# A linear-attention block: q tiles spread over the state stage, the first normaliser block inside it, and the folded Wo written to memory and read back by head groups

## Chip, cores, metric

One core of one Trainium2 chip. The metric is the device time of one execution in microseconds (us), the median of several. The profile's *span*, from the first to the last instruction, is a little shorter than the time. Positions "at 79.4" are us from the start of the span. TensorE multiplies, VectorE (DVE) and ScalarE (ACT) do elementwise work, and the sync engine's queue (SPq) issues most transfers.

## The reference, cut to what matters

```python
B, S, D = 1, 2048, 640;  H = 32;  Dh = 20
q, k, v = split(x @ wqkv)                    # [B, H, S, Dh] each
phi = lambda t: where(t > 0, t + 1, exp(t)) + 1e-6
pq, pk = phi(q), phi(k)
kv  = einsum("bhsd,bhse->bhde", pk, v)       # the state, per head
z   = einsum("bhsd->bhd", pk)
num = einsum("bhqd,bhde->bhqe", pq, kv)
den = einsum("bhqd,bhd->bhq", pq, z)[..., None] + 1e-6
out = (num / den merged over heads) @ wo
```

## The kernel before

It never forms v. TensorE computes K and phi(K) (16 tiles, `k_tile`), then the state stage `P = x^T phi(K)` in two halves of 16 steps (`p_step`), then `kv = Wv^T P` for groups of 6 heads (`kv_group`), and multiplies each group's kv into its rows of Wo (`w2_group`). This *folded Wo* is copied to the tile `w2g`, written to a DRAM buffer `w_rows`, and read back with its rows in another order into `w2p`: the *Wo round trip*. phi(Q) is made in 20 *q tiles* (`q_tile`: five 512-column matmuls, an exp on ScalarE, two VectorE operations) that fill gaps. The normaliser of each of four blocks of 512 rows is a small matmul (`den`), a reciprocal on ScalarE (`den_act`), a spreading matmul (`den_spread`), and five multiplications on VectorE (`normalize`). The sums over phi(K) that z needs are made on VectorE too (the *z additions*), and P is copied out of its banks into `pt`. At the end come 16 output tiles, each of which needs all of `w2p`.

Semaphore waits are derived from what each operation reads and writes. Every engine runs its list in order, and so does the issuing queue: an issue that waits holds back every issue behind it.

```python
# ... cut: loads, z additions, kv_group
def w2_rows():                      # after the last w2_group
    P.add("sp", lambda e: e.dma_start(
        w2d[0:5 * GW, :].rearrange("(g p) n -> p g n", p=GW),
        w2g[0:GW, 0:5 * D].rearrange("p (g n) -> p g n", n=D)), ..., dma=True)
    P.add("sp", lambda e: e.dma_start(w2d[5 * GW:D, :], w2g[0:gsz[5], 5 * D:6 * D]), ...)
    for c in range(NC_):            # five reads, 128 partitions each
        P.add("sp", lambda e, c=c: e.dma_start(
            w2p[:, c * D:(c + 1) * D],
            w2d.rearrange("(h c j) n -> c h j n", c=NC_, j=4)[c]), ..., dma=True)

# ... cut: the schedule. 16 warm-up matmuls on zeros, 16 K tiles, then
for h in range(2):
    for st in range(NT):
        p_step(h, st)
        if zst and st % 2 == 1:
            zst.pop(0)()            # one z addition on VectorE
        if st == 7:
            next_q(5 + qi[0] % 3)   # one q tile
    p_out(h)                        # evacuates banks 0..4: 3 copies ACT, 2 DVE ("pt")
    next_q(...); next_q(...)
kv_group(0)
# ... cut: six w2_groups among six q tiles, then w2_rows(); eight more q tiles
#          with den, den_spread and normalize of blocks 1 and 2; 16 output tiles
```

## Time and profile before

| | before |
|---|---|
| time, median of 4 | 110.6 us (110.52 to 110.74) |
| span of the profiled run | 109.2 us |
| first K matmul | 8.04 us |
| last matmul ends | 106.43 us |
| TensorE idle in between | 3.64 us |
| last w2g copy ends, w2p complete | 71.78, 81.32 us |

The last two rows come from the trace: the copy's record, and the last completion increment of the last read.

From the profile's page of before, its span in 40 slices, busy share in tenths (PEclk: granted TensorE clock in tenths):

```profile
PE   5949999999979999999999999994999879999990
...
PEclk9999999999999999999999999999999999999999
DMA  1999999999991000000000000074550131333333
```

TensorE is full nearly everywhere; the clock is full; the transfers come at the start and again from slice 26 (the Wo round trip and the stores). So TensorE bounds this kernel, and a change that removes no matmul can win only idle time. The timeline of TensorE of before shows that idle time: start, duration, engine, line, operation, and in brackets the idle time just before it and what ended it.

```profile
8.04 21.89 PE L237 MATMUL ps<-wk,xT 128*128 128x320 bf16 x160 [1.43 <-DMA xT<-in_x_dram]
...
30.59 5.61 PE L261 MATMUL ps<-pk,xn 128*128 128x320 bf16 x40 [0.66 <-DVE pk L252]
...
75.36 3.41 PE L287 MATMUL ps<-xT,wqp 128*128 128x512 bf16 x14 [1.52 <-DVE pq L300]
...
82.56 2.88 PE L446 MATMUL ps<-w2p,pq 128*128 128x320 bf16 x20
...
88.59 17.83 PE L446 MATMUL ps<-w2p,pq 128*128 128x320 bf16 x130 [0.68 <-ACT rd L430]
```

The first output tile (82.56) follows q work without a gap: the round trip is hidden, by a margin of 1.2 us. The queue's timeline of before has it as two writes and five reads:

```profile
70.47 0.34 SPq L387 DMA_DIRECT2D w_rows<-w2g  x1
71.81 0.29 SPq L391 DMA_DIRECT2D w_rows<-w2g  x1
76.05 3.16 SPq L395 DMA_DIRECT2D w2p<-w_rows  x5
```

### The profile page before, as it was taken

Reading aid. Unit: us, or ns where it says so; the run is one execution under the profiler, and the core shown is the slowest. Engines: PE = TensorE matmul, PEld = TensorE weight load, DVE = VectorE, ACT = ScalarE, POOL = GpSimd, SP = SyncE. Lnnn points to the kernel's source line nnn. Section 1 sums busy time; section 2 is a strip of 40 time slices with the busy share of each in tenths; the row PEclk is TensorE's granted clock in tenths of the full one; section 3 lists DMA queues with packets and bytes.
Section 4 is the critical chain, followed back from the end, with each engine's and each line's share of the span. In section 5 each row is a group of like instructions: output and inputs, shape, how many; then the busy total and the mean of one; then the engine's idle time right before and its main releaser. Section 6 shows DMA issues by size and latency. Waiting matters only on the chain.

```text
span 109.2 us, 1857 instructions
## 1 busy us (share of the span) xinstructions
PE 100.1 (92%) x738; PEld 64.2 (59%) x744; DVE 66.7 (61%) x132; ACT 41.4 (38%) x77; POOL 10.2 (9%) x25
## 2 busy tenths in 40 slices
PE   5949999999979999999999999994999879999990
PEld 2317777777657676576766756451446557777760
DVE  1002888888899899910306675899879674333331
ACT  3102555555520203400107269873566543333330
POOL 7870000480000000000000000000000000000000
PEclk9999999999999999999999999999999999999999
DMA  1999999999991000000000000074550131333333
GB/s 32 242 270 264 221 190 253 382 362 363 314 199 42 0 0 0 3 0 0 6 0 0 3 0 0 6 178 122 145 155 0 50 136 60 120 120 120 127 121 118
DMA packets 19499, 12.90 MB, mean 118 GB/s; under 512 B 10915, under 2 KB 19491, under 8 KB 19491
## 3 DMA queue, kind: packets, MB, share of 16 engines
q1 hardware_dynamic: 18178, 11.96, 39.7%
q10 hardware_dynamic: 1312, 0.82, 2.8%
q8 instruction: 6, 0.10, 0.4%
q14 instruction: 3, 0.02, 0.1%
HBM read 6.72 MB, written 3.44 MB: 93 GB/s over the span
## 4 chain that ended last, share of the span: by engine, by line
PE 72%; DVE 13%; DMA 6%; ACT 5%; issue 1%
PE ps L237 19%; PE ps L446 18%; PE ps L261 15%; PE ps L287 15%; DMA xT<-in_x_dram 6%; DVE za L306 4%; DVE pq L300 3%; ACT eq L295 3%; DVE pq L437 2%; PE ps L405 2%; PE ps L356 1%; DVE eq L297 1%; ACT rd L430 1%; PE ps L337 1%; PE ps L377 1%
## 5 line engine op out<-in xcount | busy, mean ns | idle before, releaser
L287 PE MATMUL ps<-xT,wqp 128*128 128x512 bf16 x94 | 22.9, 379 | 1.8 <-DVE pq L300 1.5
L237 PE MATMUL ps<-wk,xT 128*128 128x320 bf16 x160 | 21.9, 299 | 1.4 <-DMA xT<-in_x_dram 1.4
L261 PE MATMUL ps<-pk,xn 128*128 128x320 bf16 x160 | 22.4, 299 | 0.8 <-DVE pk L252 0.7
L446 PE MATMUL ps<-w2p,pq 128*128 128x320 bf16 x160 | 22.2, 299 | 0.7 <-ACT rd L430 0.7
L237 PEld LDWEIGHTS ps<-wk,xT 128*128 128x128 bf16 x160 | 15.6, 98 | 7.9 <-issue 1.9
L261 PEld LDWEIGHTS ps<-pk,xn 128*128 128x128 bf16 x160 | 15.5, 98 | 7.9 <-DVE pk L252 1.0
L295 ACT ACTIVATE eq<-ps 128x512 bf16<-128x512 f32 x20 | 11.9, 597 | 21.4 <-PE ps L287 21.3
L446 PEld LDWEIGHTS ps<-w2p,pq 128*128 128x128 bf16 x160 | 15.5, 98 | 7.0 <-ACT rd L430 0.8
L247 ACT ACTIVATE ek<-ps 128x640 bf16<-128x640 f32 x16 | 11.3, 704 | 16.3 <-PE ps L237 16.3
L287 PEld LDWEIGHTS ps<-xT,wqp 128*128 128x128 bf16 x100 | 9.3, 98 | 11.0 <-DVE pq L300 1.9
L455 DVE CAST osb<-ps 128x320 bf16<-128x320 f32 x16 | 7.8, 490 | 11.5 <-PE ps L446 11.5
L300 DVE SCALAR_TENSOR_TENSOR pq<-ps,eq 128x512 bf16<-128x512 f32 x20 | 13.8, 692 | 0.7
L252 DVE SCALAR_TENSOR_TENSOR pk<-ps,ek 128x640 bf16<-128x640 f32 x16 | 13.2, 825 | 0.5
L297 DVE TENSOR_SCALAR eq<-eq 128x512 bf16<-128x512 bf16 x20 | 5.8, 292 | 10.9 <-ACT eq L295 10.4
L249 DVE TENSOR_SCALAR ek<-ek 128x640 bf16<-128x640 bf16 x16 | 5.4, 339 | 11.5 <-ACT ek L247 11.3
L453 ACT CAST osb<-ps 128x320 bf16<-128x320 f32 x16 | 6.8, 426 | 13.2 <-PE ps L446 13.1
L437 DVE TENSOR_TENSOR pq<-pq,rd 128x512 bf16<-128x512 bf16 x20 | 7.0, 418 | 0.3 <-ACT rd L430 0.3
L228 PE MATMUL ps<-zero 128*128 128x512 bf16 x16 | 5.3, 509 | 1.3 <-DVE eps L149 1.3
L273 ACT CAST pt<-ps 128x320 bf16<-128x320 f32 x6 | 2.2, 434 | 9.7 <-PE ps L261 9.7
L306 DVE TENSOR_TENSOR za<-pk 128x1280 f32<-128x1280 bf16 x4 | 5.7, 1484 | 0.0
L220 POOL COPY wqp<-wqn 128x640 bf16<-128x640 bf16 x5 | 3.6, 756 | 12.7 <-DMA wqn<-in_wqkv_dram 12.7
L306 DVE TENSOR_TENSOR za<-za 128x1280 f32<-128x1280 f32 x3 | 4.4, 1487 | 0.0
(35 smaller groups left out, 39.9 us busy)
## 6 DMA issues: line engine op xcount, KB each, us to landing
xn<-in_x_dram SPq DMA_DIRECT2D x4, 640.0 KB, 9.1
out_dram<-osb SPq DMA_DIRECT2D x16, 160.0 KB, 1.8
wk<-in_wqkv_dram ACTq DMA_DIRECT2D x2, 400.0 KB, 5.5
wqn<-in_wqkv_dram SPq DMA_DIRECT2D x1, 800.0 KB, 5.2
wv<-in_wqkv_dram SPq DMA_DIRECT2D x1, 800.0 KB, 13.3
w2p<-w_rows SPq DMA_DIRECT2D x5, 160.0 KB, 2.7
wog<-in_wo_dram SPq DMA_DIRECT2D x1, 750.0 KB, 13.9
w_rows<-w2g SPq DMA_DIRECT2D x1, 750.0 KB, 5.3
```

Source lines behind the costliest of these rows:

```text
L237: r = e.matmul(bank(b + h, HALF), xT[:, c * S + 128 * st:c * S + 128 * st + 128], wk[:, c * D + HALF * h:c * D + HALF * (h + 1)], start=(c ...
L247: P.add("act", lambda e: e.activation(fold(t[:, :]), two_banks(b), ACTF.Exp), reads=banks + ["table"], writes=[("ek", st % 3)])
L252: P.add("dve", lambda e: e.scalar_tensor_tensor(fold(pk[:, st * D:(st + 1) * D]), two_banks(b), 0.0, fold(t[:, :]), ALU.max, ALU.add), rea ...
L261: r = e.matmul(bank(d, HALF), xn[:, st * D + 128 * d:st * D + 128 * d + 128], pk[:, st * D + HALF * h:st * D + HALF * (h + 1)], start=(st ...
L287: r = e.matmul(bank(b), wqp[:, d * D + 128 * c:d * D + 128 * c + 128], xT[:, d * S + BK * sbk:d * S + BK * (sbk + 1)], start=(d == 0), sto ...
L295: P.add("act", lambda e: e.activation(t[:, :], bank(b), ACTF.Exp), reads=[("bank", b), "table"], writes=[("eq", i)])
L297: P.add("dve", lambda e: e.tensor_scalar(t[:, :], t[:, :], 1.0, 1e-6, ALU.min, ALU.add), reads=[("eq", i)], writes=[("eq", i)])
L300: P.add("dve", lambda e: e.scalar_tensor_tensor(pq[:, c * S + BK * sbk:c * S + BK * (sbk + 1)], bank(b), 0.0, t[:, :], ALU.max, ALU.add), ...
L306: P.add("dve", lambda e: e.tensor_tensor(d_ap, a, b, ALU.add), reads=ra + rb, writes=[dst])
L437: P.add("dve", lambda e, v=v: e.tensor_tensor(v, v, rd[i][:, :], ALU.mult), reads=[("rd", i), ("pq", sbk, c)], writes=[("pq", sbk, c)])
L446: r = e.matmul(bank(b + h, HALF), pq[:, c * S + 128 * st:c * S + 128 * st + 128], w2p[:, c * D + HALF * h:c * D + HALF * (h + 1)], start=( ...
L455: P.add("dve", lambda e: e.tensor_copy(osb[j][:, HALF:D], bank(b + 1, HALF)), reads=[("bank", b + 1)], writes=[("osb", j, 1)])
```

## The change

Its intent: spread the q tiles over the state stage so that VectorE's work on them is even, do the first block's normaliser there, hand the normalising multiplications out one per q tile, and start the Wo round trip earlier, group by group. The edit holds more than its summary: x rows 0 to 255 now come by plain loads and are transposed on TensorE, with fewer warm-up matmuls; and the mask step stores kv with its columns in another order, so that a group's folded rows come out as five runs of 24.

```diff
+        NPE = 2          # cut: x tiles 0, 1 loaded first, transposed on TensorE,
+                         # K tiles 0, 1 done half by half; warm(16) -> warm(5), warm(4)
-        def w2_rows():   # cut, see above
+        def w2_write(g):
+            w = gsz[g] // NC_
+            P.add("sp", lambda e: e.dma_start(
+                w2d.rearrange("(c r) n -> c r n", c=NC_)[:, 24 * g:24 * g + w, :],
+                w2g[0:gsz[g], g * D:(g + 1) * D]), reads=[("w2g", g)], ..., dma=True)
+        def w2_read(g):
+            w = gsz[g] // NC_
+            P.add("sp", lambda e: e.dma_start(
+                w2p[24 * g:24 * g + w, :].rearrange("p (c n) -> p c n", n=D),
+                w2d.rearrange("(c r) n -> r c n", c=NC_)[24 * g:24 * g + w]),
+                reads=[("w2d", g)], ..., dma=True)
@@ the schedule, cut @@
+        p_step(0, 0, range(4)); p_step(0, 1, range(4))    # bank 4 later
+        p_step(0, 0, (4,));     p_step(0, 1, (4,))
+        for st in range(2, NT):
+            p_step(0, st)
+            if st % 2 == 1: zst.pop(0)()
+            if st in (3, 6, 9, 12): next_q()
+        p_out(0); next_q(); next_q()
+        for st in range(NT):
+            p_step(1, st)
+            if st == 3: z_finish(take())
+            if st == 6: inverse(0)       # den and den_act of block 0
+            if st == 9: spread(0)
+            if st in (4, 7, 10, 12): next_q()   # each also does one normalising piece
+        p_out(1); next_q(); next_q()
+        kv_group(0); next_q()
+        w2_group(0, 2); w2_write(0); inverse(1); next_q()
+        w2_group(1, 0); w2_write(1); w2_read(0)
+        w2_group(2, 2); w2_write(2); w2_read(1); spread(1); next_q()
+        w2_group(3, 0); w2_write(3); w2_read(2)
+        w2_group(4, 2); w2_write(4); w2_read(3); next_q()
+        w2_group(5, 0); w2_write(5); w2_read(4); w2_read(5)
+        # cut: four q tiles, den and spread of block 2, then the output tiles
```

More of the change, by code (lines that the diff above doesn't have):

```diff
@@ L124, in bass_standalone__linear_attn_block__prompt_kernel @@
         eps = sb("eps", 8, F32)
+        ident = sb("ident", 128)
         zero = sb("zero", BK)
@@ L147, in pool_const @@
             P.add("dve", lambda e: e.memset(zero[:, :], 0.0), writes=["zero"])
+            P.add("pool", lambda e: e.memset(ident[:, :], 0.0), writes=["ident"])
+            P.add("pool", lambda e: e.affine_select(
+                out=ident[:, :], in_=ident[:, :], pattern=[[-1, 128]], base=0,
+                channel_multiplier=1, compare_op=ALU.not_equal, fill=1.0),
+                reads=["ident"], writes=["ident"])
             P.add("dve", lambda e: e.memset(ones[:, :], 1.0), writes=["ones"])
@@ L172, in pool_const @@
                      0 if lo else DH - 1, 1 if lo else -1, "bm")
-        XCH = [(0, 256), (256, 512), (512, 1024), (1024, 1536), (1536, 2048)]
+        NPE = 2
+        XCH = [(0, 128), (128, 256), (256, 512), (512, 1024), (1024, 1536), (1536, 2048)]
         def xch_of(row):
@@ L179, in load_xT, with transpose_x, mm @@
         def load_xT():
-            for i, (a, b) in enumerate(XCH):
+            for i, (a, b) in enumerate(XCH[NPE:]):
                 P.add("sp", lambda e, a=a, b=b: e.dma_start_transpose(
                     xT[:, :].rearrange("p (c s) -> p c s", s=S)[:, :, a:b], x[0, a:b, :]),
-                    writes=[("xT", i)], dma=True)
+                    reads=[("xn", 0)] if i == 0 else [],
+                    writes=[("xT", NPE + i)], dma=True)
+        def transpose_x(st, b):
+            v = bank(b, HALF).bitcast(BF16)
+            def mm(e):
+                for c in range(NC_):
+                    r = e.transpose(v[:, 128 * c:128 * c + 128],
+                                    xn[:, st * D + 128 * c:st * D + 128 * c + 128], ident[:, :])
+                return r
+            P.add("pe", mm, reads=[("xn", st), "ident"], writes=[("bank", b)])
+            P.add("dve", lambda e: e.tensor_copy(
+                xT[:, :].rearrange("p (c s) -> p c s", s=S)[:, :, 128 * st:128 * st + 128],
+                v.rearrange("p (c s) -> p c s", s=128)),
+                reads=[("bank", b)], writes=[("xT", st)])
         def xT_keys(a, b):
@@ L192, in w_cols, with load_xn @@
                 writes=[key], dma=True)
+        def load_xn(a, b, eng):
+            P.add(eng, lambda e: e.dma_start(
+                xn[:, a * D:b * D].rearrange("p (t n) -> p t n", n=D),
+                x[0, 128 * a:128 * b, :].rearrange("(t p) n -> p t n", p=128)),
+                writes=[("xn", t) for t in range(a, b)], dma=True)
         def load_wk():
+            for t in range(NPE):
+                load_xn(t, t + 1, "act")
             w_cols(wk, 0, HALF, D, ("wk", 0), "act")
@@ L203, in load_rest @@
             w_cols(wqn, 0, D, 0, "wqn", "sp")
-            for q in range(4):
-                P.add("sp", lambda e, q=q: e.dma_start(
-                    xn[:, 4 * q * D:4 * (q + 1) * D].rearrange("p (t n) -> p t n", n=D),
-                    x[0, 512 * q:512 * (q + 1), :].rearrange("(t p) n -> p t n", p=128)),
-                    writes=[("xn", q)], dma=True)
+            for a, b in ((NPE, 4), (4, 8), (8, 12), (12, 16)):
+                load_xn(a, b, "sp")
             w_cols(wv, 0, D, 2 * D, "wv", "sp")
@@ L228, in warm, with k_half, mm, k_phi @@
                 P.add("pe", lambda e: e.matmul(
-                    bank(7), zero[:, 0:128], zero[:, :], start=True, stop=True),
-                    reads=["zero"], writes=[("bank", 7)])
-        def k_tile(st):
+                    bank(4), zero[:, 0:128], zero[:, :], start=True, stop=True),
+                    reads=["zero"], writes=[("bank", 4)])
+        def k_half(st, h):
             b = 2 * (st % 4)
-            for h in range(2):
-                def mm(e, h=h):
-                    for c in range(NC_):
-                        r = e.matmul(
-                            bank(b + h, HALF),
-                            xT[:, c * S + 128 * st:c * S + 128 * st + 128],
-                            wk[:, c * D + HALF * h:c * D + HALF * (h + 1)],
-                            start=(c == 0), stop=(c == NC_ - 1))
-                    return r
-                P.add("pe", mm, reads=xT_keys(128 * st, 128 * st + 128) + [("wk", h)],
-                      writes=[("bank", b + h)])
+            def mm(e):
+                for c in range(NC_):
+                    r = e.matmul(
+                        bank(b + h, HALF),
+                        xT[:, c * S + 128 * st:c * S + 128 * st + 128],
+                        wk[:, c * D + HALF * h:c * D + HALF * (h + 1)],
+                        start=(c == 0), stop=(c == NC_ - 1))
+                return r
+            P.add("pe", mm, reads=xT_keys(128 * st, 128 * st + 128) + [("wk", h)],
+                  writes=[("bank", b + h)])
+        def k_phi(st):
+            b = 2 * (st % 4)
             banks = [("bank", b), ("bank", b + 1)]
@@ L255, in k_tile, with p_step @@
                 reads=banks + [("ek", st % 3)], writes=[("pk", st)])
-        def p_step(h, st):
+        def p_step(h, st, ds=range(NC_)):
             def mm(e):
-                for d in range(NC_):
+                for d in ds:
                     r = e.matmul(
@@ L265, in mm @@
                 return r
-            P.add("pe", mm, reads=[("xn", st // 4), ("pk", st)],
-                  writes=[("bank", d) for d in range(NC_)])
+            P.add("pe", mm, reads=[("xn", st), ("pk", st)],
+                  writes=[("bank", d) for d in ds])
         def p_out(h):
@@ L364, in kv_group @@
                       writes=[("bank", bb)])
-            for lo, n, bb, w, key in ((0, 4, b, GW, 0), (4, 1, b + 1, GW, 1), (5, 1, b + 1, 40, 2)):
-                src = ps[0:w, BK * bb + 128 * (lo % 4):BK * bb + 128 * (lo % 4) + 128 * n] \
-                    .rearrange("p (g j) -> p g j", j=128)[:, :, 0:w]
-                mk = bm[0:w, 0:w].unsqueeze(1).broadcast_to([w, n, w])
-                dst = kvt[0:w, GW * lo:GW * (lo + n)].rearrange(
-                    "p (g j) -> p g j", j=GW)[:, :, 0:w]
+            for g in range(NG):
+                bb, w, nh = b + g // 4, gsz[g], gsz[g] // DH
+                src = ps[0:w, BK * bb + 128 * (g % 4):BK * bb + 128 * (g % 4) + w].rearrange(
+                    "p (h c j) -> p h c j", c=NC_, j=4)
+                mk = bm[0:w, 0:w].rearrange("p (h c j) -> p h c j", c=NC_, j=4)
+                dst = kvt[0:w, GW * g:GW * g + w].rearrange("p (c h j) -> p h c j", h=nh, j=4)
                 P.add("dve", lambda e, src=src, mk=mk, dst=dst: e.tensor_tensor(
-                    dst, src, mk, ALU.mult), reads=[("bank", bb), "bm"], writes=[("kvt", key)])
+                    dst, src, mk, ALU.mult), reads=[("bank", bb), "bm"], writes=[("kvt", g)])
         def w2_group(g, b):
@@ L379, in w2_group @@
                     wog[0:n, g * D + HALF * h:g * D + HALF * (h + 1)], start=True, stop=True),
-                    reads=[("kvt", 0 if g < 4 else g - 3), "wog", "wog5"],
+                    reads=[("kvt", g), "wog", "wog5"],
                     writes=[("bank", b + h)])
@@ L384, in w2_group @@
                 reads=[("bank", b), ("bank", b + 1)], writes=[("w2g", g)])
-        def w2_rows():
+        def w2_write(g):
+            w = gsz[g] // NC_
             P.add("sp", lambda e: e.dma_start(
-                w2d[0:5 * GW, :].rearrange("(g p) n -> p g n", p=GW),
-                w2g[0:GW, 0:5 * D].rearrange("p (g n) -> p g n", n=D)),
-                reads=[("w2g", g) for g in range(5)], writes=["w2d"], dma=True)
-            P.add("sp", lambda e: e.dma_start(
-                w2d[5 * GW:D, :], w2g[0:gsz[5], 5 * D:6 * D]),
-                reads=[("w2g", 5)], writes=["w2d5"], dma=True)
-            for c in range(NC_):
-                P.add("sp", lambda e, c=c: e.dma_start(
-                    w2p[:, c * D:(c + 1) * D],
-                    w2d.rearrange("(h c j) n -> c h j n", c=NC_, j=4)[c]),
-                    reads=["w2d", "w2d5"], writes=[("w2p", c)], dma=True)
+                w2d.rearrange("(c r) n -> c r n", c=NC_)[:, 24 * g:24 * g + w, :],
+                w2g[0:gsz[g], g * D:(g + 1) * D]),
+                reads=[("w2g", g)], writes=[("w2d", g)], dma=True)
+        def w2_read(g):
+            w = gsz[g] // NC_
+            P.add("sp", lambda e: e.dma_start(
+                w2p[24 * g:24 * g + w, :].rearrange("p (c n) -> p c n", n=D),
+                w2d.rearrange("(c r) n -> r c n", c=NC_)[24 * g:24 * g + w]),
+                reads=[("w2d", g)], writes=[("w2p", g)], dma=True)
         def den(sbk, b):
@@ L431, in den_spread, with normalize, out_tile @@
                   reads=[("bank", b)], writes=[("rd", i)])
-        def normalize(sbk):
+        def normalize(sbk, c):
             i = sbk % 2
-            for c in range(NC_):
-                v = pq[:, c * S + BK * sbk:c * S + BK * (sbk + 1)]
-                P.add("dve", lambda e, v=v: e.tensor_tensor(v, v, rd[i][:, :], ALU.mult),
-                      reads=[("rd", i), ("pq", sbk, c)], writes=[("pq", sbk, c)])
-        def out_tile(st):
-            b = 2 * (st % 4)
+            v = pq[:, c * S + BK * sbk:c * S + BK * (sbk + 1)]
+            P.add("dve", lambda e: e.tensor_tensor(v, v, rd[i][:, :], ALU.mult),
+                  reads=[("rd", i), ("pq", sbk, c)], writes=[("pq", sbk, c)])
+        def out_tile(st, b):
             j = st % 4
@@ L451, in out_tile @@
                 P.add("pe", mm, reads=[("pq", st // 4, c) for c in range(NC_)]
-                      + [("w2p", c) for c in range(NC_)], writes=[("bank", b + h)])
+                      + [("w2p", g) for g in range(NG)], writes=[("bank", b + h)])
             P.add("act", lambda e: e.copy(osb[j][:, 0:HALF], bank(b, HALF)),
@@ L459, in out_tile @@
                 reads=[("osb", j, 0), ("osb", j, 1)], writes=[("out", st)], dma=True)
+        pool_const()
         load_wk()
         load_xT()
-        pool_const()
         load_rest()
         permute_wq()
-        warm(16)
-        for st in range(NT):
-            k_tile(st)
+        warm(5)
+        for st in range(NPE):
+            transpose_x(st, 6 + st)
+        warm(4)
+        for h in range(2):
+            for st in range(NPE):
+                k_half(st, h)
+        for st in range(NPE):
+            k_phi(st)
@@ L470, in bass_standalone__linear_attn_block__prompt_kernel @@
+        for st in range(NPE, NT):
+            k_half(st, 0)
+            k_half(st, 1)
+            k_phi(st)
         zst = z_steps()
         qs = [(s, c) for s in range(NSB) for c in range(NC_)]
-        qi = [0]
-        def next_q(b):
-            q_tile(*qs[qi[0]], b)
-            qi[0] += 1
-        for h in range(2):
-            for st in range(NT):
-                p_step(h, st)
-                if zst and st % 2 == 1:
-                    zst.pop(0)()
-                if st == 7:
-                    next_q(5 + qi[0] % 3)
-            p_out(h)
-            next_q(5 + qi[0] % 3)
-            next_q(5 + qi[0] % 3)
+        todo = []
@@ new lines, in bass_standalone__linear_attn_block__prompt_kernel, with take, next_q, inverse @@
+        small = [5, 6, 7]
+        def take():
+            small.append(small.pop(0))
+            return small[-1]
+        def next_q(n=1):
+            q_tile(*qs.pop(0), take())
+            for _ in range(n):
+                if todo:
+                    todo.pop(0)()
+        def inverse(sbk):
+            b = take()
+            den(sbk, b)
+            den_act(sbk, b)
+        def spread(sbk):
+            den_spread(sbk, take())
+            todo.extend(lambda c=c: normalize(sbk, c) for c in range(NC_))
@@ L488, in bass_standalone__linear_attn_block__prompt_kernel @@
+        p_step(0, 0, range(4))
+        p_step(0, 1, range(4))
+        p_step(0, 0, (4,))
+        p_step(0, 1, (4,))
+        for st in range(2, NT):
+            p_step(0, st)
+            if st % 2 == 1:
+                zst.pop(0)()
+            if st in (3, 6, 9, 12):
+                next_q()
+        p_out(0)
+        next_q()
+        next_q()
         for f in zst:
             f()
+        for st in range(NT):
+            p_step(1, st)
+            if st == 3:
+                z_finish(take())
+            if st == 6:
+                inverse(0)
+            if st == 9:
+                spread(0)
+            if st in (4, 7, 10, 12):
+                next_q()
@@ L490, in bass_standalone__linear_attn_block__prompt_kernel @@
+        p_out(1)
+        next_q()
+        next_q()
         kv_group(0)
-        next_q(5)
-        z_finish(4)
+        small[:] = [5, 6, 7, 4]
+        next_q()
         w2_group(0, 2)
-        next_q(6)
+        w2_write(0)
+        inverse(1)
+        next_q()
         w2_group(1, 0)
-        den(0, 4)
-        den_act(0, 4)
-        next_q(7)
+        w2_write(1)
+        w2_read(0)
         w2_group(2, 2)
-        den_spread(0, 4)
-        next_q(5)
+        w2_write(2)
+        w2_read(1)
@@ L502, in bass_standalone__linear_attn_block__prompt_kernel @@
+        spread(1)
+        next_q()
         w2_group(3, 0)
-        normalize(0)
-        next_q(6)
+        w2_write(3)
+        w2_read(2)
         w2_group(4, 2)
-        next_q(7)
+        w2_write(4)
+        w2_read(3)
+        next_q()
         w2_group(5, 0)
-        den(1, 4)
-        w2_rows()
-        den_act(1, 4)
-        next_q(5)
-        next_q(6)
-        den_spread(1, 4)
-        normalize(1)
-        while qi[0] < 15:
-            next_q((7, 2, 3, 5, 6)[qi[0] % 5])
-        next_q(0)
@@ L518, in bass_standalone__linear_attn_block__prompt_kernel @@
-        next_q(1)
-        den(2, 4)
-        den_act(2, 4)
-        next_q(2)
-        next_q(3)
-        den_spread(2, 4)
-        normalize(2)
-        next_q(5)
-        for st in range(2):
-            out_tile(st)
-        den(3, 6)
-        den_act(3, 6)
-        out_tile(2)
-        den_spread(3, 6)
-        normalize(3)
-        for st in range(3, NT):
-            out_tile(st)
+        w2_write(5)
+        w2_read(4)
+        w2_read(5)
+        next_q()
+        inverse(2)
+        next_q()
@@ L536, in bass_standalone__linear_attn_block__prompt_kernel @@
+        next_q()
+        spread(2)
+        next_q()
+        out_tile(0, 0)
+        for f in todo[:2]:
+            todo.pop(0)()
+        out_tile(1, 2)
+        while todo:
+            todo.pop(0)()
+        inverse(3)
+        out_tile(2, 0)
+        out_tile(3, 2)
+        small[:] = [7]
+        spread(3)
+        for st in range(4, NT):
+            out_tile(st, 2 * (st % 4) if st > 5 else 2 * (st % 2))
+            if todo:
+                todo.pop(0)()
         block = es(nc.Block())
```

## The prediction

> **What bounds the kernel now.** TensorE. In the timeline of the kernel before, the last matmul ends at 106.4 us of a 109.2 us span; from the first K matmul (8.04) on, TensorE idles only about 3.5 us: 0.66 (at 30.6), 1.52 (75.4), 0.32 (85.8), 0.68 (88.6) and small ones. The chain of waits begins with 7.1 us of the transposing load of x. The change removes no matmul of the algorithm, so only idle time can be won.
>
> **Piece by piece.**
> 1. *Start.* The edit has parts that its summary leaves out: x rows 0 to 255 come by plain loads ahead of wk and are transposed on TensorE; warm-up matmuls fall from 16 to 9. Before, wk's first half landed at 5.05 us, its second and the first xT chunk at 7.9. After (estimate from those packet rates): x lands near 3.3 and 3.7, wk near 5.3 and 7.1, the first transposed chunk near 8. K tile 2 starts near 8.5 instead of 10.8; K ends 2.2 us earlier. If the clock is still half when K starts (before, it rose at 4.8 us, after steady matmuls from 1.26), only 1.2. The Trainium skill, "TensorE: Matmul & The Clock Gate" (The HAM clock gate), gives about 3.4 us of busy time for warming; the trace's 3.5 us agrees.
> 2. *K to P.* The first P steps leave bank 4 to later: the 0.66 us wait goes.
> 3. *State stage.* In its first half VectorE has, in order, seven z additions (1.42 to 1.48 us each), six q tiles (0.93) and two pt copies, and waits for early q tiles between additions. I count pt done 18.8 us after K's end, TensorE ready at 17.4: a new stall of 1.4 us.
> 4. *Normaliser.* Work unchanged; one normalising piece per q tile removes the 1.52 and 0.68 us waits.
> 5. *Wo round trip.* Before, it took 9.6 us from the last w2g copy (71.8) to w2p landed (81.3), hidden under 11.6 us of TensorE time. Now about 5 us of TensorE work follows the last w2 group. The queue issues in order: write g+2 behind read g, which waits for write g. The write's pattern is 5x24 rows against 120; the skill, "DMA: Bandwidth & Descriptors" (Why a DMA increments its semaphore by 16), says the engine count divides both outermost sizes: 5. The before trace agrees for 120 against 120 rows (15 completions) and 40 (10). With 24 rows per engine at 54 to 100 ns, I estimate 2.9 to 3.6 us per write, three in a row, then the last read: w2p lands 8 us after the last w2g copy. The first output tile waits 3 to 5 us, which may also halve the clock for a while.
>
> **Sum.** -2.2 (start), -0.7, +1.4, -2.5 (old waits), +4 (w2p), +0.4 (clock): near zero; less if writes run faster than I count. **Predicted 109.3 us, range 106.0 to 111.4.** Faster by over 2%: 0.36; within 2%: 0.56; slower: 0.08.
>
> **What would show it.** First K matmul near 5.3, K end near 27.7; a TensorE idle of 1.4 us put down to VectorE's pt copy; an idle of 3 to 5 us before the first output tile put down to the DMA of w2p; writes of w2_rows with 5 completions and about 3 us to landing; no waits at pq in the q stage.
>
> **What would make it wrong.** Writes spread over more engines (w2p's stall 2 us or less, time about 107); a cold clock at K's start or after the w2p gap (towards 111).

## The result

| | before | after |
|---|---|---|
| time, median of 4 | 110.6 us | 117.3 us (116.03 to 117.64) |
| span of the profiled run | 109.2 us | 115.4 us |
| mean granted clock | 1.000 | 0.956 |
| first K matmul | 8.04 us | 6.03 us |
| last matmul ends | 106.43 us | 112.62 us |
| TensorE idle in between | 3.64 us | 9.55 us |
| last w2g copy ends, w2p complete | 71.78, 81.32 us | 75.39, 87.15 us |

The ratio of after to before is 1.058 (interval 1.050 to 1.066). Ratios here are the mean time of one kernel's fast runs over that of the other's of the same rounds, so not quite the ratio of the medians.

The page of after, its 40 slices:

```profile
PE   5899999999999996899999999995007999999990
...
PEclk9999999999999999999999999999855589999999
```

Two empty slices in the PE line, and half clock right behind them. The timeline of TensorE of after:

```profile
6.03 21.91 PE L265 MATMUL ps<-wk,xT 128*128 128x320 bf16 x160 [0.66 <-DMA wk<-in_wqkv_dram]
...
27.77 2.88 PE L292 MATMUL ps<-pk,xn 128*128 128x320 bf16 x20
...
46.55 2.89 PE L292 MATMUL ps<-pk,xn 128*128 128x320 bf16 x20 [1.27 <-DVE pt L307]
...
78.19 1.24 PE L318 MATMUL ps<-xT,wqp 128*128 128x512 bf16 x5
87.28 5.49 PE L477 MATMUL ps<-w2p,pq 128*128 128x320 bf16 x20 [7.85 <-DMA w2p<-w_rows]
...
93.21 2.89 PE L477 MATMUL ps<-w2p,pq 128*128 128x320 bf16 x20
```

Read from the top: K starts 2.0 us earlier; the 0.66 us wait between K and P is gone; a wait of 1.27 us for the pt copies has come before the second half of P; the waits at pq are gone; and the first output tile waits 7.85 us for w2p. Its first 20 matmuls then take 5.49 us, the next 20 take 2.89: half clock. A table by stretch of after (start and end, length, busy us of PE, PEld, DVE, ACT and POOL, granted clock, DMA share, GB/s) shows the same, no TensorE work and then work at half clock:

```profile
80.00:87.00 7.00, 0.00 (x0) 0.00 (x0) 1.55 (x4) 0.06 (x1) 0.00 (x0) 0.70 0.34 100
87.00:93.00 6.00, 5.72 (x36) 3.08 (x38) 1.35 (x4) 0.85 (x2) 0.00 (x0) 0.50 0.09 29
```

With the end of the last matmul as the mark, the books close. K starts 2.01 us earlier. Idle time grows by 9.55 - 3.64 = 5.91 us. TensorE is busy for 2.29 us more (112.62 - 6.03 - 9.55 = 97.04, against 94.75) on matmuls that are all but the same: that is the half clock. Together -2.01 + 5.91 + 2.29 = +6.19, which is 112.62 - 106.43.

The queue's timeline of after shows why w2p is late. L421 are writes, L428 reads:

```profile
69.78 2.55 SPq L421 DMA_DIRECT2D w_rows<-w2g  x2
73.30 0.33 SPq L428 DMA_DIRECT2D w2p<-w_rows  x1
73.68 0.70 SPq L421 DMA_DIRECT2D w_rows<-w2g  x1
75.19 0.31 SPq L428 DMA_DIRECT2D w2p<-w_rows  x1
75.55 0.70 SPq L421 DMA_DIRECT2D w_rows<-w2g  x1
78.68 0.30 SPq L428 DMA_DIRECT2D w2p<-w_rows  x1
79.03 0.70 SPq L421 DMA_DIRECT2D w_rows<-w2g  x1
80.52 0.30 SPq L428 DMA_DIRECT2D w2p<-w_rows  x1
80.87 0.70 SPq L421 DMA_DIRECT2D w_rows<-w2g  x1
83.72 1.21 SPq L428 DMA_DIRECT2D w2p<-w_rows  x2
```

The last write is issued at 80.87, though its data were ready at 75.39: it stands behind the read of group 3, which waits for the write of group 3. The chain of waits that ended last, in order of time, goes through exactly this:

```profile
75.55 4.95 DMA w_rows<-w2g
...
80.52 0.30 SPq L428
...
80.87 3.77 DMA w_rows<-w2g
...
84.66 2.49 DMA w2p<-w_rows
...
87.28 5.49 PE ps L477 x20
```

Each write's semaphore in the trace gets one early update and then five completions, against fifteen (120 rows) and ten (40 rows) for the two writes of before: five engines. From start of issue to last completion the six writes took 3.5, 3.5, 5.0, 4.95, 4.7 and 3.8 us.

### The profile page after: what moved, and what is told of

The parts are those of the page before. It is cut to its first block, busy times and chain, and to the rows that moved or that the text cites. A ratio compares the mean times of both kernels' runs of the same rounds, so it can differ in the third digit from the quotient of the medians.

```text
span 115.4 us, 1877 instructions
## 1 busy us (share of the span) xinstructions
PE 101.2 (88%) x741; PEld 65.0 (56%) x747; DVE 67.6 (59%) x137; ACT 41.4 (36%) x77; POOL 10.6 (9%) x27
## 3 DMA queue, kind: packets, MB, share of 16 engines
HBM read 6.72 MB, written 3.44 MB: 88 GB/s over the span
## 4 chain that ended last, share of the span: by engine, by line
PE 77%; DMA 13%; DVE 5%; issue 1%; ACTq 1%; ACT 1%; SPq 0%
PE ps L477 21%; PE ps L265 19%; PE ps L292 17%; PE ps L318 14%; DMA w_rows<-w2g 8%; DMA wk<-in_wqkv_dram 4%; DVE za L337 3%; DMA w2p<-w_rows 2%; PE ps L409 2%; PE ps L387 1%; PE ps L438 1%; PE ps L368 1%; ACTq L218 1%; DVE pt L307 1%; DVE pq L331 1%
## 5 line engine op out<-in xcount | busy, mean ns | idle before, releaser
L477 PE MATMUL ps<-w2p,pq 128*128 128x320 bf16 x160 | 24.8, 320 | 7.9 <-DMA w2p<-w_rows 7.9
L477 PEld LDWEIGHTS ps<-w2p,pq 128*128 128x128 bf16 x160 | 16.4, 103 | 15.7 <-issue 8.3
L292 PE MATMUL ps<-pk,xn 128*128 128x320 bf16 x160 | 23.9, 299 | 1.3 <-DVE pt L307 1.3
L469 DVE TENSOR_TENSOR pq<-pq,rd 128x512 bf16<-128x512 bf16 x20 | 8.1, 416 | 0.0
L256 PE MATMUL ps<-zero 128*128 128x512 bf16 x9 | 3.3, 518 | 1.3 <-DVE eps L155 1.3
L164 POOL TENSOR_SCALAR_AFFINE_SELECT em<-em 128x128 bf16<-128x128 bf16 x8 | 4.2, 523 | 0.5
```

The source lines that it names most:

```text
L292: r = e.matmul(bank(d, HALF), xn[:, st * D + 128 * d:st * D + 128 * d + 128], pk[:, st * D + HALF * h:st * D + HALF * (h + 1)], start=(st ...
L469: P.add("dve", lambda e: e.tensor_tensor(v, v, rd[i][:, :], ALU.mult), reads=[("rd", i), ("pq", sbk, c)], writes=[("pq", sbk, c)])
L477: r = e.matmul(bank(b + h, HALF), pq[:, c * S + 128 * st:c * S + 128 * st + 128], w2p[:, c * D + HALF * h:c * D + HALF * (h + 1)], start=( ...
```

## The experiments

Theory A: the write's outer size of 5 confines it to five engines, and that makes the round trip long. Rival B: the queue's order (each write behind an earlier group's read) is the cause. Rival C: too little TensorE work is left after the last w2 group to hide any round trip. "Trip" below is the time from the end of the last w2g copy to w2p complete, "gap" the TensorE idle before the first output tile. Some runs of one kernel are longer at a lower mean clock; where one was classed as slow it is left out of ratios, and kernels are compared here by their fast runs. A time marked *all runs* still contains the slow one.

**e1_contig**: each group goes to 120 consecutive rows, and the read reorders. Nothing else differs.

```diff
-  w2d.rearrange("(c r) n -> c r n", c=NC_)[:, 24 * g:24 * g + w, :],
+  w2d[GW * g:GW * g + gsz[g], :],
...
-  w2d.rearrange("(c r) n -> r c n", c=NC_)[24 * g:24 * g + w]),
+  w2d[GW * g:GW * g + gsz[g], :].rearrange("(c r) n -> r c n", c=NC_)),
```

> Edit: each group's rows are written to 120 consecutive rows of w2_rows, and the read does the reordering; order of the queue, number of transfers and bytes stay. Theory A (the write's outer size 5 confines it to 5 of 16 engines): writes show 15 completions and land in about 2 us instead of 3.5 to 5.0; w2p is complete about 4.5 us after the last w2g copy (near 80); the idle before the first output tile falls from 7.9 us to under 1.5, the clock stays full, time 106 to 108 us. Rival B (the queue's order, write g+2 behind read g): gap stays above 4 us, time above 111. Rival C (too little TensorE work left to hide any round trip): gap of 4 us or more, time above 111.

Measured: 110.37 us in the fast runs (110.84 in all runs), ratio to before 1.001 (0.996 to 1.007). Fifteen completions per write (ten for the last), trip 7.3 us (after: 11.8), gap 3.42 us. The TensorE timeline of e1_contig at the first output tile:

```profile
83.23 2.88 PE L477 MATMUL ps<-w2p,pq 128*128 128x320 bf16 x20 [3.42 <-DMA w2p<-w_rows]
```

In the fast runs two lines of indexing bring the ratio from 1.058 back to 1.001, and the gap from 7.85 to 3.42 us, so A holds for the larger part. But the gap fits neither side of what was expected: not under 1.5, not above 4. And the writes took 2.0 us only for the first two; later ones, in flight with reads, took 2.7 to 3.3. In the profiled run the clock stayed full across this gap; one of the fast runs shows a mean clock of 0.984, and the run classed slow (113.04 us) one of 0.969.

**e2_near_five**: outer size 5 kept, but the five runs of 24 rows lie 25 rows apart instead of 128.

```diff
-  w2d.rearrange("(c r) n -> c r n", c=NC_)[:, 24 * g:24 * g + w, :],
+  w2d[125 * g:125 * g + 125, :].rearrange("(c r) n -> c r n", r=25)[:, 0:w, :],
```

> Edit: the write keeps its outer size of 5 but its five blocks of 24 rows lie almost back to back (25 rows apart instead of 128). Theory A (outer size 5): 5 completions, landing 3.5 to 5 us, gap about 7.9 us, time 116 to 118. Rival (rows scattered over DRAM are slow): landing about 2 us, time about 107.

Measured: 115.66 us, five completions, writes 3.3 to 4.9 us (the first 3.5), trip 11.0, gap 7.0 us. Rows lying close do not help, so the scatter over memory is not the cause. The time is a little under the range; the half clock lasted 6.8 us instead of 10.2.

**e3_writes_first**: all six writes are issued before the six reads, with five engines as in after.

> Edit: all six writes are issued before the six reads, so no write waits behind a read; the writes keep 5 engines. Theory A (five engines are the limit): the 128 rows per engine still take about 8 to 9 us from 70.5, the last write lands near 80 to 81, w2p near 83.5 to 84.5, gap 4 to 5 us, time 112 to 115. Rival B (queue order is the whole cost): gap under 2 us, time about 107. If the order does no harm: 117.

Measured: 113.84 us, last write landed at 81.05, trip 9.0, gap 4.97 us. The TensorE timeline of e3_writes_first:

```profile
84.92 4.56 PE L477 MATMUL ps<-w2p,pq 128*128 128x320 bf16 x20 [4.97 <-DMA w2p<-w_rows]
```

This is what A expected, and it gives B a share too: order cost the five-engine trip 2.8 us.

**e4_block_trip**: before's round trip, and its mask step that goes with it, in after's schedule.

> Edit: the Wo round trip of the kernel before (two writes after the last w2g copy, five reads) in the schedule of after. Theory (cover was lost, and the trip by groups made it worse still): w2p complete about 9.6 us after the last w2g copy (75.4), near 85; gap 5 to 6 us, half clock after it for 2 or 3 windows of 3.4 us; time 113 to 116, thus faster than after's 117.3. If the trip by groups were at least no worse than the block: 117 or above.

Measured: 115.68 us, trip 9.9, gap 5.96 us. The TensorE timeline of e4_block_trip:

```profile
85.76 5.49 PE L476 MATMUL ps<-w2p,pq 128*128 128x320 bf16 x20 [5.96 <-DMA w2p<-w_rows]
```

Before's own trip, hidden in before, sticks out by 6 us here: so C is real. And the trip by groups made the gap 1.9 us longer than the block trip would have.

**e5_fill**: after, with dummy matmuls in the gap.

```diff
+        warm(34, 7)          # 34 matmuls on zeros into bank 7
         out_tile(0, 0)
```

> Edit: after, plus 34 dummy matmuls on zeros (7.3 us at full clock) between the last q tile and the first output tile, inside the idle of 7.9 us. Theory (the idle lets the clock fall to half for 2 or 3 windows of 3.4 us, which costs 1.7 to 2.9 us of output matmuls): granted clock 1.0 in every run, first 20 output matmuls 2.9 us instead of 5.5, time 113.5 to 115, and less spread between runs. If the clock fall had another cause: half clock stays, 117.

Measured: 115.34 us (114.96 to 115.84), ratio 1.043. Clock 0.997 to 1.0 in all four runs, and the spread fell to 0.9 us. The TensorE timeline of e5_fill:

```profile
79.87 7.51 PE L256 MATMUL ps<-zero 128*128 128x512 bf16 x34
88.67 2.88 PE L477 MATMUL ps<-w2p,pq 128*128 128x320 bf16 x20 [1.29 <-DMA w2p<-w_rows]
```

The half clock came from the idle. Filling it with useless work wins 1.7 us by the means of the runs (117.07 against 115.37), the low end of the 1.7 to 2.9 expected; in the profiled run the trip itself was 0.6 us longer.

**e6_front_only**: before with only the new start.

> Edit: before, with only the start of after (x rows 0 to 255 by plain loads and TensorE transposes, 9 warm-up matmuls, halves of K tiles 0 and 1 reordered). Theory: K ends near 28.0 instead of 30.0 and all of it is kept, because TensorE paces what follows: time 108.0 to 109.0, ratio 0.98 to 0.985. If the gain is given back by a later wait on loads: within 0.5 us of before.

Measured: 109.18 us (108.95 to 109.67), ratio 0.989 (0.986 to 0.992). In the profiled run, 108.98 us, K starts at 5.96 and the last matmul ends at 104.48 instead of 106.43: there all of the 2.0 us is kept. The median gain is smaller, 1.3 us, than expected. Why other runs gain less is not shown, since they have no profile.

**e7_contig_first**: e1 and e3 together.

> Edit: e1 (consecutive rows) and e3 (all writes issued before the reads) together. Theory D (engine count and queue order each hold the trip, and the rest is missing cover): last write issued at 75.8 instead of 77.6, all reads issued by about 79, w2p complete near 81, gap 1.0 to 2.0 instead of 3.4 us, clock full in every run, time 107.5 to 109. Rival (transfers in flight together slow one another so that the order is worth nothing): gap 3 us or more, time 110 to 111.

Measured: 112.96 us in the fast runs (113.15 in all runs), ratio 1.021 (1.015 to 1.027): slower than e1. The theory missed. The writes were now quick (2.0 us each, the last landed at 77.36), but the six reads, issued 0.42 us apart from 76.17, landed at 78.86, 79.80, 80.83, 82.03, 82.55 and 82.94. Trip 7.1, gap 3.32 us, as in e1. The chain of e7_contig_first shows the last read, of a third of the others' size, taking 4.70 us because of those before it:

```profile
78.23 4.70 DMA w2p<-w_rows
...
83.18 5.49 PE ps L477 x20
```

So with fifteen engines the order is worth nothing: what the writes gain the reads lose. A full-size read follows the one before it by 0.92 us on average (3.69 us over four; singly 0.52 to 1.20). The Trainium skill, "SBUF — State Buffer" (Door 1: The DMA port swizzle), says that bandwidth depends on how many of 16 ports the partitions reach, 27.2 GB/s each. By its formula 24 partitions reach 6. Estimate from that page: 153.6 KB over 6 x 27.2 GB/s take 0.94 us. The average here is near it, but that does not show that the ports are the cause: the reads are in flight together, each full-size one shows twelve completions and not sixteen, and in e3 reads of the same size into the same partitions landed 0.69 us apart (2.76 us over four). The difference to e1 is the clock: the first 20 output matmuls took 5.49 us here and 2.88 in e1's profile, after gaps of 3.32 and 3.42 us. Why so like a gap cost clock in one profile and not in the other is taken up under point 6 below; it is not to be read as an effect of the order.

**e8_z_later**: e7, and the last two z additions of the first half come after the pt copies.

```diff
-            if st % 2 == 1:
+            if st % 2 == 1 and st < 12:
                 zst.pop(0)()
 ...
-            if st == 3: z_finish(take())    # cut: inverse at 6, spread at 9
+            if st == 7: z_finish(take())    # inverse at 9, spread at 11
```

> Edit: e7, and the last two z additions of the first half come after the pt copies, with z_finish, den and spread of block 0 four, three and two P steps later. Theory (VectorE's order holds the pt copies back): the 1.27 us TensorE idle before the second half vanishes, all later work comes 1.2 to 1.3 us earlier, time 1.0 to 1.4 us under e7's. If the idle has another cause: no change, or the wait moves to z_finish.

Measured: 111.43 us, ratio 1.008 (1.006 to 1.011), 1.4 us under e7 by the means of the fast runs (111.39 against 112.76). The 1.27 us wait is gone from the profile, so it was VectorE's order. The gain lies within the expected 1.0 to 1.4; the gap became 3.7 us, and the runs differ in how long the clock was halved.

**e9_hold_three**: e8 with three q tiles taken out of the state stage and done after the last w2 group; den and spread of block 1 also come a little later.

```diff
-            if st in (3, 6, 9, 12): next_q()     # first half
+            if st in (3, 7, 11): next_q()
-            if st in (4, 7, 10, 12): next_q()    # second half
+            if st in (4, 10): next_q()
 ...
         w2_group(5, 0); w2_write(5)
         for g in range(NG): w2_read(g)
+        next_q(); next_q(); next_q()             # cut: then den of block 2, four more
```

> Edit: e8, with three q tiles taken out of the state stage (nine in it instead of twelve) and done after the last w2 group instead, 3 x 1.09 = 3.3 us of TensorE work behind which the round trip can hide; den and spread of block 1 one or two pieces later. Theory (what is left of the gap, 3.3 to 3.7 us in e1, e7 and e8, is missing cover): gap under 0.8 us, clock 1.0 in every run; against before the start gives -2.0 (1.3 in time in e6), K to P -0.7, old waits -2.5, so time 104.5 to 106.5, ratio 0.945 to 0.965. Rival (the trip stretches because it runs beside q work, or a new wait for banks appears): gap of 2 us or more, time above 108.

Measured: 106.32 us (106.13 to 106.45), ratio 0.9617 (0.9600 to 0.9634), clock 0.997 to 1.0 in all five runs. The waits of TensorE in e9_hold_three (who waited for whom: total us, times, longest) have no w2p any more:

```profile
PE ps L256 <- DVE eps L155: 1.3, 1, 1.3
PE ps L438 <- DVE pq L331: 1.0, 1, 1.0
PE ps L265 <- DMA wk<-in_wqkv_dram: 0.4, 1, 0.4
```

The TensorE timeline of e9_hold_three has the first output tile with no wait before it:

```profile
79.21 2.88 PE L477 MATMUL ps<-w2p,pq 128*128 128x320 bf16 x20
```

The trip is no shorter (7.5 us); it is hidden. The last matmul ends at 101.83.

**e10_block_reads**: e4, with each group's 120 consecutive rows written at once and before's five reads of 128 partitions after the last write.

> Edit: e4, but each group's 120 consecutive rows are written as soon as it is copied, and the five reads of 128 partitions follow the last write, as in before. Theory (early writes over 15 engines help, reads by head group do not): last write lands near 77.4, reads issued at 0.6 us each, w2p near 82.7, gap about 3 us as in e7, and time 110 to 113 according to whether the clock drops. If reads by group were worth something: gap well above 3.4 us.

Measured: 111.93 us, last write landed at 77.45, w2p complete at 82.91, trip 7.0, gap 3.20 us. Reading by head group is worth nothing here: five full reads, all after the last write, end when e7's six narrow ones do.

**e11_den_later**: e9 with den of block 2 two q tiles later and its spread after the last one.

> Edit: e9 with den of block 2 two q tiles later (its last pq pieces were not ready: 1.0 us TensorE idle in e9) and its spread after the last q tile. Theory: that idle goes and nothing else moves, time 105.0 to 105.7, ratio 0.950 to 0.957. If VectorE, not the place of den, paces this stretch: the wait moves to a later q tile or to the output tiles and the time stays at 106.3.

Measured: 106.15 us (105.99 to 106.39), ratio 0.961 (0.959 to 0.963): not separable from e9. The wait at den vanished and the first output tile now waits 0.93 us for w2p. The time stayed, as the rival said, but for a third reason: the round trip was just behind.

**e12_hold_five**: e9 with after's own round trip.

> Edit: e9 with the Wo round trip as in after (writes of outer size 5, each read between the writes). Tells whether cover alone repairs the change. Theory (the trip of after takes 11.8 us from the last w2g copy to w2p, about 7.5 are covered in e9's schedule): gap 3 to 5 us, clock at half for one or two windows, time 110 to 113. If lost cover was the whole cause: gap under 1 us, time about 106.5.

Measured: 110.87 us in the fast runs (111.22 in all runs), ratio 1.003 (0.996 to 1.010). The profiled run was classed slow (111.67 us, clock 0.984); two of the three fast runs have the same clock. Its trip is 11.6 us and its gap 3.44. Cover, with the z additions moved, brings after back to before; fifteen engines and writes first are worth another 4.5 us (fast runs, 110.87 against 106.32).

## Why the prediction was wrong

Its range of 106.0 to 111.4 us did not hold 117.3. Point by point:

1. *Start, -2.2 us*: K starts 2.01 us earlier and ends at 27.94 instead of 29.93. Right, though the first K matmul came at 6.03 and not near 5.3, since the first half of wk landed at 5.98. Alone, over several runs, it is worth 1.3 us (e6).
2. *K to P, -0.7*: right; the wait is gone.
3. *State stage, +1.4*: 1.27 us, put down to the pt copy as foretold; e8 removes it by VectorE's order alone.
4. *Old waits, -2.5*: right; the waits of 1.52, 0.32 and 0.68 us are gone.
5. *Wo round trip, +4, and clock, +0.4*: here the prediction failed. The mechanism was right: five engines, and write g+2 behind read g behind write g. The Trainium skill, "DMA: Bandwidth & Descriptors" (Why a DMA increments its semaphore by 16), gives the rule, and the trace agrees with five completions. The sizes were wrong. The step was "I estimate 2.9 to 3.6 us per write, three in a row, then the last read: w2p lands 8 us after the last w2g copy". The first two writes took 3.5 us, inside the estimate; the three after them, in flight with other writes and reads, took 4.7 to 5.0, and the last, with only eight rows per engine, still 3.8. The trip measured 11.8 us and the gap 7.85, not 3 to 5. That transfers in flight stretch one another shows also with fifteen engines: 2.0 us per write among writes (e7), up to 3.3 among reads (e1).
6. The clock was put at +0.4 and cost 2.3. The same skill's "TensorE: Matmul & The Clock Gate" (What's actually happening) lets the clock fall after at least one idle window of about 3.4 us, and says that the windows run freely: they do not begin with the idle. The traces agree on the windows. In all 13 profiles that hold clock records (e5's holds none), every fall comes a whole number of windows of 3.41 us after the clock's first rise (after: rise at 4.23, fall at 82.74, 23 windows). They differ on how much idle it takes. In after, 3.31 us of the window that ended at 82.74 were idle; but in e7 2.05 us of a window were enough (idle from 79.86, fall at 81.91), and no fall in any profile came after less. In e1 a window boundary at 81.27 split the gap of 3.42 us into 1.46 and 1.96 us, and the clock stayed full: that was luck, since its gap was the longer one. Estimate from these figures: a wait of 3 to 4 us costs clock or not by where it falls, and one above 4.1 us always does. So the prediction should have given its wait of 3 to 5 us more weight. The half clock lasted 10.24 us, and e5 shows that the idle caused it.

The prediction's terms add up to +0.4 us, and its centre was put 1.3 us under before in case the writes were faster. With +7.85 and +2.3 in the places of +4 and +0.4 they add up to +6.15; the last matmul came 6.19 us later.

What caused the loss, in shares of the gap: against before, whose trip was hidden with 1.2 us to spare, moving q tiles forward uncovered a trip of before's kind by 6.0 us (e4); writing by groups over five engines in this order made it 7.85; the same groups over fifteen engines leave 3.4 (e1); and three q tiles moved back, with the writes first and the z additions moved, hide that too (e9).

Left open: why the start alone keeps less than its 2.0 us in some runs (not shown; in the profiles with the new start K ends between 27.9 and 28.5, and where the clock's first rise is recorded it comes between 4.23 and 6.81), and how much of a late write's stretch comes from other writes and how much from reads. Other writes can do most of it: in e3 the third write took 4.4 us, and no read was issued until 0.6 us before it landed.

## What to carry to other kernels

Before work is moved forward out of a stretch, ask what was hiding behind it: evening out one engine's load cost only the 1.27 us at the pt copies by itself, but it uncovered a memory round trip. When a transfer is cut into pieces, look at the outermost size of both sides of each piece: here an outer 5 undid more than the earlier start won. And keep each wait of TensorE under 2 us where you can: here no window with up to 1.96 us of idle cost clock, and every one with 2.05 us or more did.

## What the Trainium skill lacked or had wrong

- "TensorE: Matmul & The Clock Gate" has the clock fall after at least one idle window of about 3.4 us. Less was enough here: the clock fell after windows with 2.05 us of idle (e7, fall at 81.91; e9 after its last matmul, 101.83 to 103.88) and not after one with 1.96 us (e1). The halved stretches came in whole windows: 3.41 us (e3, e10, e12), 6.83 (e2, e4, e7, e8) and 10.24 (after).
- "DMA: Bandwidth & Descriptors" gives the rule for the engine count but no measured time for a transfer so confined: 120 rows of 1280 bytes from SBUF to memory took 3.5 us over 5 engines (the first write of after) and 2.0 us over 15 (e7), and issuing the 5 x 24 write held the queue for 0.70 us against 0.32.
- No page has times for small transfers that are in flight together: the five-engine write went from 3.5 to 5.0 us (after), the fifteen-engine one from 2.0 to 3.3 (e1).
